# Four layers of linear attention and MLP on one Trainium2 core: the order of VectorE's first instructions, and three more row tiles turned by DMA

## The chip, the core and the metric

The kernel runs on one core of a Trainium2 chip. The core has TensorE (matrix products, into PSUM), VectorE, ScalarE and GpSimd (elementwise work), and SyncE, whose queue issues all DMAs of this kernel. The metric is the device time of one execution in microseconds (us). Every time in this text is in us unless another unit stands beside it.

## The reference

`x` is a bf16 array of 2048 rows by 576 columns. Two kinds of layer follow each other in the order A, B, A, B, each with a residual sum:

```python
def A(x, wqkv, wo):                      # 32 heads of 18 columns
    q, k, v = split(x @ wqkv)
    phi = lambda t: where(t > 0, t + 1, exp(t)) + 1e-6
    pq, pk = phi(q), phi(k)
    kv  = einsum("bhsd,bhse->bhde", pk, v)
    z   = einsum("bhsd->bhd", pk)
    num = einsum("bhqd,bhde->bhqe", pq, kv)
    den = einsum("bhqd,bhd->bhq", pq, z) + 1e-6
    return merge_heads(num / den) @ wo

def B(x, w1, b1, w2, b2):                # 576 -> 4608 -> 576
    y = layernorm(x)
    return gelu(y @ w1 + b1) @ w2 + b2

x = x + A(layernorm(x)); x = x + B(layernorm(x))
x = x + A(layernorm(x)); x = x + B(layernorm(x))
```

In the original, `A` gets `layernorm(x)`; B gets `layernorm(x)` too and applies a layernorm of its own to it, so B's rows are normalised twice. Both A layers use the same weights, and both B layers.

## The kernel before

The 2048 rows are 16 tiles of 128 rows. Layers are numbered from 1 in this text; in the code `li` counts from 0, so layer 1 is `li == 0`. Every product needs normalised rows with the model's columns on the partitions. That turned copy is `yT`, 128 partitions by 5 chunks by 2048 rows. A row tile becomes part of `yT` in three ways, named by `evac`: `"act"` (five TensorE transposes into PSUM, line 494, and a ScalarE copy, line 500, or for tiles 0 and 1 one copy each on ScalarE and VectorE, lines 497 and 498), `"xbar"` (one DMA transpose from SyncE's queue, line 483), and `"dma"` (VectorE's 32x32 transposes and a trip through DRAM, used for later layers).

`LNPipe` is a pipeline of normalisations. `feed` puts a tile in, and each `tick` takes every tile one stage on: stage 0 takes the statistics, on VectorE (two `bn_stats`, lines 391 and 392, an aggregate, line 398) or with `stats="act"` on ScalarE (a sum by Identity, line 371, a sum of squares by Square, line 381, and a small GpSimd step, line 384); stage 1 the inverse root, stage 2 the scale and shift, stage 3 the normalisation, stage 4 the turn. TensorE transposes are emitted by a tick with `transposes=1` only; a tick with `transposes=0` takes on everything else. `hold` is a number of ticks that a tile waits, and for tiles of a B layer `tp_at` is the number of the output tile (`state["wo"]`) ahead of which it isn't turned.

Layer 1 begins with a stretch written out by hand: the norms and keys of tiles 0 to 3 (`k_half(t, half)`: keys of one tile, half of the 576 columns; line 657), sums of rows times keys (`rows_by_keys`, line 699; its chunk 4 goes to a tile `k_tail` of its own), and the first two q products (`q_proj`, line 625: five matmuls for one group of heads and 512 rows). The products of q and k go through an exp on ScalarE (lines 544, 558, 559) and one or two VectorE instructions (546, 564, 566). TensorE's order is the order of emission (`pe_chain`). On the other engines the compiler's scheduler chooses, within data dependencies and manual edges. `in_order` lays such edges over VectorE's and ScalarE's first instructions by short names: `s2a`, `s2b`, `g2`, `u2` are the two statistics, the aggregate and the variance step of tile 2; `n2` its normalisation (line 440 for tiles 0 to 3, on VectorE; later tiles have it on GpSimd, line 436); `cd1` VectorE's copy of turned tile 1; `ma10` the VectorE step that finishes keys of tile 1, half 0; `e10` its exp and `ca1` ScalarE's copy.

Then a loop over tiles 4 to 15 repeats: keys of tile t, feed and tick (`pre_a1_layer0`, which also issues one piece of the weights for later, `late_pieces`), the row sums of tile t - 1, one q product, a tick without transposes. Tiles 0 to 7 (`XB = 8`) are turned by TensorE, tiles 8 to 15 by DMA. ScalarE takes the statistics of tiles 9, 12 and 15. The turn DMAs of layer 1 and all loads of weights are `chained`: SyncE issues them in order of emission.

The output stage of layer 1 is a loop over 16 output tiles: `wo_stage(t)` multiplies (ten matmuls, line 968, into one of two PSUM bank pairs), `residual` adds the input rows on VectorE (line 609) and stores the sum to DRAM from SyncE's queue (line 616). The first four sums are fed to the pipeline as layer 2's rows of block 0 (kind "B", normalised on GpSimd, line 457, into one of three ring buffers). They are turned by TensorE after output tiles 6, 10, 11 and 14. From output tile 12 on, each step issues one of the last three pieces of `w2` (`last_pieces`, 864 KB each). Layer 2's MLP begins with block 0, all of whose four row tiles its first product needs (line 1082).

Of the kernel before, what the change touches and what calls it, by code (L numbers as in the profile page):

```python
# [15 lines left out]
P = 128  # L16
NT = S // P
KD = 5
DPAD = KD * P
# [8 lines left out]
TPC = CB // P  # L28
# [8 lines left out]
def build(tc, A_x, A_wqkv, A_wo, B_w1, B_b1, B_w2, B_b2, out, dbg=None, n_layers=4):  # L37
    nc = tc.nc
    dbg = dbg or {}
    with ExitStack() as ctx:  # L40
# [90 lines left out]
        yT = const.tile([P, KD, S], BF16, name="yT")  # L131
# [3 lines left out]
        y_ring = [const.tile([P, DPAD], BF16, name=f"y_ring{i}") for i in range(NY)]  # L135
        key_eps = const.tile([P, 8], F32, name="key_eps")
        AHEAD = 4
        XB = 8
        turned = const.tile([P, D // 32, TPC, 32], BF16, name="turned")
        x_d = dpool.tile([NT, P, D], F32, name="x_d")  # L140
        yrow_d = dpool.tile([NCB, 4, TPC, 32, D], BF16, name="yrow_d")
# [197 lines left out]
        class LNPipe:  # L339
# [11 lines left out]
            def tick(self, transposes=1):  # L351
                land()
                for it in list(self.items):
                    st = it["stage"]
                    if st == 4 and it["evac"] not in ("dma", "xbar"):
                        if transposes == 0 or state["wo"] < it["tp_at"]:
                            continue
                        transposes -= 1
# [3 lines left out]
                    if st == -1:  # L362
                        xn = row_tile("xl")
                        load = nc.sync.dma_start(out=xn[:], in_=x_d[it["load"]])
                        if it["after"] is not None:
                            tc.add_manual_dep(load.ins, it["after"], NOSYNC, reason="loads give way")
                        it["xt"] = xn
                    elif st == 0 and it["stats"] == "act":
                        mv = it["mv"] = work.tile([P, 2], F32, name="ln_mv", bufs=6)
                        it["dump"] = blk.tile([P, D], BF16, name="ln_dump", tag="blk")  # L370
                        one = nc.scalar.activation(out=it["dump"][:], in_=it["xt"][:, 0:D], func=ACT.Identity,
                                                   scale=-1.0 / D, accum_out=mv[:, 0:1])
                        if it["after"] == "rden":
                            tc.add_manual_dep(one.ins, act_last["copy"], NOSYNC, reason="scalings first")
                        it["stage"] = 0.5
                        if it["kind"] == "B":
                            continue
                    if it["stage"] == 0.5:
                        u = it["u"] = work.tile([P, 1], F32, name="ln_u", bufs=4)
# [94 lines left out]
                    elif st == 4:  # L474
                        t = it["t"]
                        first_layer = it["kind"] == "A" and it["evac"] in ("act", "xbar")
                        y = it["xt"] if first_layer else it["y"]
                        if it["evac"] == "dma":
                            turn_rows(y, t, it["kind"])
                            self.items.remove(it)  # L480
                            continue
                        if it["evac"] == "xbar":
                            chained(nc.sync.dma_start_transpose(out=yT[:, :, t * P:(t + 1) * P], in_=y[:, 0:DPAD]))
                            self.items.remove(it)
                            continue
                        tp = ps_h.tile([P, 512], F32, name="tp", tag="h")
                        tp = tp[:, 0:DPAD // 2].bitcast(BF16).rearrange("p (k n) -> p k n", k=KD)
                        first = first_layer and t < 2
                        tp2 = tp
                        if first:  # L490
                            tp2 = ps_h.tile([P, 512], F32, name="tp2", tag="h")
                            tp2 = tp2[:, 0:DPAD // 2].bitcast(BF16).rearrange("p (k n) -> p k n", k=KD)
                        for k in range(KD):
                            pe(nc.tensor.transpose(out=(tp if k < 3 else tp2)[:, k, :], in_=y[:, k * P:(k + 1) * P],
                                                   identity=ident[:]))
                        if first:
                            named(f"ca{t}", nc.scalar.copy(out=yT[:, 0:3, t * P:(t + 1) * P], in_=tp[:, 0:3, :]))  # L497
                            named(f"cd{t}", nc.vector.tensor_copy(out=yT[:, 3:KD, t * P:(t + 1) * P], in_=tp2[:, 3:KD, :]))
                        elif it["evac"] == "act":
                            turned_tile = nc.scalar.copy(out=yT[:, :, t * P:(t + 1) * P], in_=tp)  # L500
                            act_last["turned"] = turned_tile.ins.name
                            if first_layer and t < 5:
                                named(f"ca{t}", turned_tile)
                            elif act_last["exp"] is not None:
                                tc.add_manual_dep(turned_tile.ins, act_last["exp"], NOSYNC, reason="keys go on first")
                        else:
                            nc.vector.tensor_copy(out=yT[:, :, t * P:(t + 1) * P], in_=tp)
                        self.items.remove(it)
                        continue
# [6 lines left out]
        lnp = LNPipe()  # L516
# [102 lines left out]
        def layer_A(li, next_kind, pre_a1=None):  # L619
# [237 lines left out]
            if li == 0:  # L857
# [5 lines left out]
                def feed_and_tick(t, n):  # L863
                    feed0(t, after=dve_last["phi"] if t > 5 else None)
                    for _ in range(n):
                        lnp.tick()
# [13 lines left out]
                k_half(3, 1)  # L880
                k_half(3, 0)
                q_proj(*q_left.pop(0))
                phi = q_proj(*q_left.pop(0), defer=True)
                feed_and_tick(5, 1)
                feed_and_tick(6, 2)
                phi(after=first_ones["ca4"].ins.name)
                in_order("s0a s0b g0 s1a s1b n0 g1 cd0 n1 s2a s2b g2 cd1 s3a ma00 n2 s3b g3 u3 ma10 s4a "
                         "n3 ma11 ma20 s4b ma21 g4 u4 ma01 s5a s5b g5 u5 ma30 ma31")
                in_order("ln0 re0 ln1 re1 ca0 e00 ca1 ln2 re2 e01 e10 ca2 e11 e20 e21 ca3 e31 e30 ca4")
                rows_by_keys(3, 0, (0, 1, 2, 3), done=False)  # L890
                for t in range(4):
                    rows_by_keys(t, 0, (4,))
                for t in range(4, NT):
                    keys(t)
                    pre_a1(t)
                    if t == 4:
                        lnp.tick()
                    masks(2)
                    if t > 4:
                        rows_by_keys(t - 1, 0)  # L900
                    q_proj(*q_left.pop(0), defer=True)(after=act_last["turned"])
                    lnp.tick(transposes=0)
                q_proj(*q_left.pop(0))
# [68 lines left out]
            def wo_stage(t):  # L972
                wo_products(t, range(wo_open[t][0] if t in wo_open else 0, G))
                wp = wo_open[t][1]
                xn = residual(li, t, wp[:, :, 0:HALF])
                if xn is not None and next_kind == "B" and t < TPC:
                    lnp.feed(xn, t, "B", "pool", "act", hold=(2, 5, 6, 8)[t] if li > 0 else (2, 8, 8, 10)[t], tp_at=6 + 2 * t if li > 0 else (6, 10, 11, 14)[t],
                             **(dict(after="sum") if t in (0, 3 if li > 0 else 2) else dict(stats="act", after="rden")))

            for t in range(AHEAD if li == 0 else AHEAD + 2):  # L980
# [14 lines left out]
            for t in range(NT):  # L995
# [17 lines left out]
                    quad_stage((t + 1) // 2, after=total)  # L1013
                if t == NT - 3:
                    warm_table(ACT.Gelu_apprx_tanh, act_last["copy"])
                if last_pieces and t >= NT - TPC:
                    last_pieces.pop(0)()
                state["wo"] = t
                lnp.tick()
                if t < 10:  # L1020
# [12 lines left out]
        class LayerB:  # L1033
# [70 lines left out]
            def run(self):  # L1104
# [7 lines left out]
                for c in range(NCB):  # L1112
# [2 lines left out]
                        tc.add_manual_dep(zero.ins, act_last["gelu"], NOSYNC, reason="not urgent")  # L1115
                    for g in range(self.done.get(c, 0), NGRP):
                        self.m1_group(c, g)
                        if g in (3, 5):
                            prefetch_xo(li, c * TPC + (g - 3) // 2, add_b2=True)
                        if g in (2, 3, 4, 5):  # L1120
                            feed_next(c, g - 2)
                        lnp.tick(transposes=0)
                        lnp.tick(transposes=0)
# [37 lines left out]

        def feed0(t, after=None):
            lnp.feed(x0_tiles.pop(t), t, "A", l0_norm_eng(t), "act" if t < XB else "xbar", after=after,
                     stats="act" if t >= XB and t % 3 == 0 else "dve")

        pe_chain.update(on=True, last=None)
        warm_pe(9)
# [7 lines left out]
        warm_pe(2)  # L1175

        def pre_a1_layer0(t):
            for ahead in (3, 4) if t == 4 else (4,):
                if t + ahead < NT:
                    feed0(t + ahead, after=dve_last["phi"])  # L1180
            lnp.tick()
            if late_pieces:
                late_pieces.pop(0)()
            if t == NT - 1:
                piece_b2_dma()
                while late_pieces:
                    late_pieces.pop(0)()
# [67 lines left out]
```

## Time and profile before

| what | value |
|---|---|
| median of 3 runs | 758.32 (758.32 to 758.42) |
| the profiled execution | 759.16 |
| its span, first to last instruction | 757.2 |
| granted TensorE clock, mean | 0.999 of full speed |
| TensorE busy | 750.6 (99% of the span) |
| VectorE, ScalarE, GpSimd busy | 261.3, 323.3, 114.9 |
| layer 1 up to its last q product, about | 0 to 60 |
| layer 1, sums and output stage | 60 to 100 |
| layer 2's first MLP product starts | 100.14 |

In rows of a timeline stand the start, the time from the first instruction's start to the last one's end, the engine, the line, the operation, what it writes and reads, its shape, and how many instructions are merged; in brackets the idle time of the engine before it and what ended that. Matmuls are pipelined, so what one costs TensorE is the distance from its start to the next start.

### The profile page before, as it was taken

The numbers are of one execution on the slowest core, as the hardware profiler recorded it, in microseconds if no ns is written. First come the engines' busy times: TensorE is split into PE (matmuls) and PEld (weight loads), VectorE is DVE, ScalarE is ACT, GpSimd is POOL, SyncE is SP. The second block draws the span as 40 slices with busy tenths as digits, with TensorE's granted clock in tenths as the row PEclk, the third lists the DMA queues.
The fourth block names the chain that finished last, engine by engine and source line by source line (L and its number), as shares of the span: only waits on it lengthen the run. The fifth ranks groups of instructions, "written<-read, shape, count | busy, mean of one in ns | idle before, by whom it ended". The sixth has DMA issues, their size and how long they took to land.

```text
span 757.2 us, 15677 instructions
## 1 busy us (share of the span) xinstructions
PE 750.6 (99%) x6555; PEld 484.7 (64%) x6555; DVE 261.3 (35%) x641; ACT 323.3 (43%) x722; POOL 114.9 (15%) x219
## 2 busy tenths in 40 slices
PE   8999999999999999999999999999999999999998
PEld 5677754774476457646777777457646754774476
DVE  7766824136034403401366567600230132000000
ACT  5767656105601640373057666660174036205600
POOL 4830313003010201200110004300020020001000
PEclk9999999999999999999999999999999999999999
DMA  8796692226313611411404147430240033011000
GB/s 241 172 246 159 200 350 65 71 65 182 82 40 94 166 51 48 121 54 32 127 24 118 32 137 256 173 83 16 87 106 17 16 126 83 9 32 56 1 9 24
DMA packets 83984, 75.20 MB, mean 99 GB/s; under 512 B 39882, under 2 KB 68554, under 8 KB 83914
## 3 DMA queue, kind: packets, MB, share of 16 engines
q1 hardware_dynamic: 83914, 74.21, 34.5%
q8 instruction: 51, 0.84, 0.5%
q14 instruction: 19, 0.16, 0.1%
HBM read 48.10 MB, written 24.77 MB: 96 GB/s over the span
## 4 chain that ended last, share of the span: by engine, by line
PE 95%; DMA 1%; ACT 1%; DVE 1%; POOL 1%; SPq 0%; issue 0%; POOLq 0%; DVEq 0%
PE m_ps L1144 36%; PE h_ps L1082 21%; PE hp_ps L1082 16%; PE q_ps L625 5%; PE k_ps L657 5%; PE k_ps L699 4%; PE wo_ps L968 3%; PE m_half L1144 1%; DMA xo<-x_d 1%; DMA x<-in_A_x_dram 1%; PE k_tail L699 0%; PE kv_ps L751 0%; ACT turned L846 0%; PE rden_ps L842 0%; PE den_ps L801 0%
## 5 line engine op out<-in xcount | busy, mean ns | idle before, releaser
L1144 PE MATMUL m_ps<-w_sb,hT 128*128 128x288 bf16 x2232 | 274.8, 286 | 0.0
L1144 PEld LDWEIGHTS <-hT 128*128 128x128 bf16 x2304 | 224.2, 98 | 60.4 <-issue 3.4
L1082 PEld LDWEIGHTS <-w_sb 64*128 64x128 bf16 x2304 | 124.5, 94 | 136.4 <-issue 1.9
L1082 PE MATMUL hp_ps<-yT,w_sb 64*128 64x512 bf16 x1152 | 178.0, 376 | 0.0
L1082 PE MATMUL h_ps<-yT,w_sb 64*128 64x512 bf16 x1152 | 148.0, 376 | 0.0
L1087 ACT COPY relay_sb<-relay_sb 128x1 f32<-128x1 f32 x144 | 28.5, 198 | 261.2 <-PE h_ps L1082 218.1
L1078 ACT ACTIVATE hT<-h_ps,b1T 128x512 bf16<-128x512 f32 x144 | 91.1, 683 | 43.8 <-PE h_ps L1082 43.8
L427 POOL TENSOR_TENSOR ln_rstd<-ln_u,neg_half 128x1 f32<-128x1 f32 x61 | 34.3, 563 | 412.3 <-DVE ln_u L409 209.4
L1078 ACT ACTIVATE hT<-hp_ps,b1T 128x512 bf16<-128x512 f32 x144 | 91.1, 692 | 0.0
L609 DVE TENSOR_TENSOR xbf<-m_ps,xo 128x576 bf16<-128x576 f32 x15 | 11.4, 757 | 212.9 <-PE m_ps L1144 212.9
L609 DVE TENSOR_TENSOR xo<-m_ps,xo 128x576 f32<-128x576 f32 x16 | 12.1, 757 | 168.2 <-PE m_ps L1144 168.2
L592 POOL TENSOR_TENSOR xo<-xo,b_bc 128x576 f32<-128x576 f32 x32 | 40.9, 1281 | 115.2 <-DMA xo<-x_d 85.3
L1082 PE MATMUL h_ps<-yT,w_tail 64*128 64x512 bf16 x144 | 54.1, 376 | 0.0
L1082 PE MATMUL hp_ps<-yT,w_tail 64*128 64x512 bf16 x144 | 54.1, 376 | 0.0
L625 PE MATMUL q_ps<-yT,wqkv_sb 128*126 128x512 bf16 (+1 forms) x200 | 49.4, 379 | 0.4 <-DVE pk L546 0.4
L657 PE MATMUL k_ps<-wqkv_sb,yT 128*128 128x288 bf16 x320 | 44.6, 286 | 0.3 <-DMA wqkv_sb<-in_A_wqkv_dram 0.2
L968 PE MATMUL wo_ps<-kvwo,pq 126*128 126x288 bf16 (+1 forms) x320 | 43.5, 286 | 0.6 <-DVE xo L609 0.4
L1082 PEld LDWEIGHTS <-w_tail 64*128 64x128 bf16 x288 | 27.1, 94 | 17.1
L657 PEld LDWEIGHTS <-yT 128*128 128x128 bf16 x320 | 31.0, 98 | 10.6 <-ACT yT L497 0.6
L968 PEld LDWEIGHTS <-pq 126*128 126x128 bf16 (+1 forms) x320 | 30.3, 97 | 9.6 <-issue 1.3
L558 ACT ACTIVATE phi_e<-q_ps 126x512 bf16<-126x512 f32 (+1 forms) x40 | 23.9, 596 | 23.6 <-PE q_ps L625 21.6
L625 PEld LDWEIGHTS <-wqkv_sb 128*126 128x126 bf16 (+1 forms) x200 | 25.7, 131 | 12.3 <-issue 1.0
(151 smaller groups left out, 562.5 us busy)
## 6 DMA issues: line engine op xcount, KB each, us to landing
xo<-x_d SPq DMA_DIRECT2D x48, 288.0 KB
x_d<-xo SPq DMA_DIRECT2D x32, 288.0 KB
xl<-x_d SPq DMA_DIRECT2D x24, 288.0 KB
y_d<-turned SPq DMA_DIRECT2D x40, 144.0 KB
w_sb<-in_B_w_dram SPq DMA_DIRECT2D x6, 864.0 KB
yT<-y_d SPq DMA_DIRECT2D x10, 512.0 KB
w_sb<-in_B_w_dram SPq DMA_DIRECT2D x9, 512.0 KB
x_d<-xn SPq DMA_DIRECT2D x16, 288.0 KB
```

Of the source, the lines that this page charges most:

```text
L427: nc.gpsimd.tensor_tensor(out=rstd[:], in0=it["u"][:], in1=neg_half[:], op=ALU.pow)
L558: exp = nc.scalar.activation(out=e_out, in_=ps_ap, func=ACT.Exp)
L592: nc.gpsimd.tensor_tensor(out=xo[:], in0=xo[:], in1=b2_bc[:], op=ALU.add)
L609: total = nc.vector.tensor_tensor(out=xn[:, cols].rearrange("p (h n) -> p h n", h=2), in0=halves, in1=xo[:, cols].rearrange("p (h n) -> p ...
L625: pe(nc.tensor.matmul(qp[0:GR[g], :], lhsT=wqkv_sb[:, k, GO[g]:GO[g] + GR[g]], rhs=yT[:, k, c * CA:(c + 1) * CA], start=(k == 0), stop=(k ...
L657: pe(nc.tensor.matmul(kp[:, 0:HALF], lhsT=yT[:, k, t * P:(t + 1) * P], rhs=wqkv_sb[:, k, D + half * HALF: D + (half + 1) * HALF], start=(k ...
L699: pe(nc.tensor.matmul(dst, lhsT=lhsT, rhs=pk, start=(t == 0), stop=(t == NT - 1)))
L968: pe(nc.tensor.matmul(wp[:, half, 0:HALF], lhsT=pq[(g, c)][0:GR[g], j * P:(j + 1) * P], rhs=kvwo[g][0:GR[g], half * HALF:(half + 1) * HALF ...
L1078: act_last["gelu"] = nc.scalar.activation(out=to, in_=ps, func=ACT.Gelu_apprx_tanh, bias=b1T[:, f:f + 1], scale=1.0).ins.name
L1082: mm = pe(nc.tensor.matmul(dst[n], lhsT=wt, rhs=mv, start=(seen[n] == 0), stop=(seen[n] == 8)))
L1087: relay = nc.scalar.copy(out=relay_sb[:, 1:2], in_=relay_sb[:, 0:1])
L1144: pe(nc.tensor.matmul(acc[half][:, 0:cols.stop - cols.start], lhsT=hT[f][:, j * P:(j + 1) * P], rhs=w2_sb[:, f, cols], start=(f == 0), sto ...
```

## The change

- `XB` goes from 8 to 7: tile 7 is turned by DMA. Its statistics move to ScalarE, and the rule `t % 3 == 1` in place of `t % 3 == 0` gives ScalarE the tiles 7, 10 and 13 instead of 9, 12 and 15.
- Tile 7 is fed ahead of the loop, with a tick without transposes, and without the edge that put its statistics behind VectorE's last key step. Tile 8 alone is fed at t = 4.
- The feeds and ticks of tiles 5 and 6 come ahead of the second q product instead of behind it, so tile 4 is turned between the first and the second.
- VectorE's order by hand is another one: among others `ma00` and `n2` go ahead of `s3a`, `ma01` moves up behind `ma10`, and the statistics of tiles 4 and 5 move down.
- The four `k_tail` products of tiles 0 to 3 come behind the keys of tile 4 instead of ahead of them.
- In layer 1's output stage, the rows of tiles 0 and 1 for layer 2's block 0 are turned by DMA (not `chained`) instead of TensorE, not ahead of output tiles 6 and 10. Tile 1's two statistics steps on ScalarE are emitted in one tick.
- The three last pieces of `w2` are issued with the first three groups of layer 2's first products instead of with output tiles 12 to 14.

```diff
-        XB = 8
+        XB = 7
...
                     st = it["stage"]
+                    if st == 4 and it["kind"] == "B" and it["evac"] == "xbar" and state["wo"] < it["tp_at"]:
+                        continue
                     if st == 4 and it["evac"] not in ("dma", "xbar"):
...
                         it["stage"] = 0.5
-                        if it["kind"] == "B":
+                        if it["kind"] == "B" and it["evac"] != "xbar":
                             continue
...
+                        if it["evac"] == "xbar" and it["kind"] == "B":
+                            nc.sync.dma_start_transpose(out=yT[:, :, t * P:(t + 1) * P], in_=y[:, 0:DPAD])
+                            self.items.remove(it)
+                            continue
                         if it["evac"] == "xbar":
...
                 q_proj(*q_left.pop(0))
-                phi = q_proj(*q_left.pop(0), defer=True)
                 feed_and_tick(5, 1)
                 feed_and_tick(6, 2)
+                phi = q_proj(*q_left.pop(0), defer=True)
+                feed0(7)
+                lnp.tick(transposes=0)
                 phi(after=first_ones["ca4"].ins.name)
-                in_order("s0a s0b g0 s1a s1b n0 g1 cd0 n1 s2a s2b g2 cd1 s3a ma00 n2 s3b g3 u3 ma10 s4a "
-                         "n3 ma11 ma20 s4b ma21 g4 u4 ma01 s5a s5b g5 u5 ma30 ma31")
+                in_order("s0a s0b g0 s1a s1b n0 g1 cd0 n1 s2a s2b g2 cd1 ma00 n2 s3a s3b g3 u3 ma10 ma01 n3 ma11 ma20 "
+                         "s4a s4b g4 u4 ma21 ma31 s5a ma30 s5b g5 u5")
                 in_order("ln0 re0 ln1 re1 ca0 e00 ca1 ln2 re2 e01 e10 ca2 e11 e20 e21 ca3 e31 e30 ca4")
                 rows_by_keys(3, 0, (0, 1, 2, 3), done=False)
-                for t in range(4):
-                    rows_by_keys(t, 0, (4,))
                 for t in range(4, NT):
                     keys(t)
                     pre_a1(t)
                     if t == 4:
-                        lnp.tick()
+                        lnp.tick(transposes=0)
                     masks(2)
                     if t > 4:
                         rows_by_keys(t - 1, 0)
+                    else:
+                        for one in range(4):
+                            rows_by_keys(one, 0, (4,))
                     q_proj(*q_left.pop(0), defer=True)(after=act_last["turned"])
...
-                    lnp.feed(xn, t, "B", "pool", "act", hold=(2, 5, 6, 8)[t] if li > 0 else (2, 8, 8, 10)[t], tp_at=6 + 2 * t if li > 0 else (6, 10, 11, 14)[t],
+                    lnp.feed(xn, t, "B", "pool", "xbar" if li == 0 and t < 2 else "act", hold=(2, 5, 6, 8)[t] if li > 0 else (2, 8, 8, 10)[t], tp_at=6 + 2 * t if li > 0 else (6, 10, 11, 14)[t],
...
-                if last_pieces and t >= NT - TPC:
-                    last_pieces.pop(0)()
...
                         self.m1_group(c, g)
+                        if last_pieces:
+                            last_pieces.pop(0)()
...
-                     stats="act" if t >= XB and t % 3 == 0 else "dve")
+                     stats="act" if t >= XB and t % 3 == 1 else "dve")
...
-            for ahead in (3, 4) if t == 4 else (4,):
-                if t + ahead < NT:
-                    feed0(t + ahead, after=dve_last["phi"])
+            if t + 4 < NT:
+                feed0(t + 4, after=dve_last["phi"])
```

## The prediction

> **What bounds the kernel now.** I read the page's shares and chain first.
>
> ```profile
> PE 750.6 (99%) x6555; PEld 484.7 (64%) x6555; DVE 261.3 (35%) x641; ACT 323.3 (43%) x722; POOL 114.9 (15%) x219
> ...
> PE 95%; DMA 1%; ACT 1%; DVE 1%; POOL 1%; SPq 0%; issue 0%; POOLq 0%; DVEq 0%
> ```
>
> TensorE is busy 750.6 of 757.2 us and is 95% of the chain, at a granted clock of 0.999. So only two things can shorten the run: fewer TensorE instructions, or its 6.6 us of idle time. The view of TensorE's waits over the whole span names most of the second:
>
> ```profile
> PE warm_ps L221 <- DVE y_ring L216: 1.3, 1, 1.3
> PE tp L494 <- DVE x L440: 0.6, 1, 0.6
> PE q_ps L625 <- DVE pk L546: 0.4, 1, 0.4
> PE wo_ps L968 <- DVE xo L609: 0.4, 1, 0.4
> PE tp L494 <- ACT phi_a L559: 0.2, 1, 0.2
> PE k_ps L657 <- DMA wqkv_sb<-in_A_wqkv_dram: 0.2, 1, 0.2
> ```
>
> The second, third and fifth lie where the diff works. TensorE's timeline (start, duration, instructions, idle time before) places them:
>
> ```profile
> 9.61 0.45 PE L494 MATMUL tp<-ident,x 128*128 128x128 bf16 x5 [0.62 <-DVE x L440]
> ...
> 16.88 0.44 PE L494 MATMUL tp<-ident,x 128*128 128x128 bf16 x5
> 17.15 0.66 PE L699 MATMUL k_ps<-pk,x 128*128 128x289 bf16 x4
> 17.65 0.66 PE L699 MATMUL k_tail<-pk,x 128*65 128x289 bf16 x4
> 18.14 1.39 PE L657 MATMUL k_ps<-wqkv_sb,yT 128*128 128x288 bf16 x10
> 19.36 0.44 PE L494 MATMUL tp<-ident,x 128*128 128x128 bf16 x5
> 20.20 1.24 PE L625 MATMUL q_ps<-yT,wqkv_sb 128*126 128x512 bf16 x5 [0.39 <-DVE pk L546]
> ...
> 26.19 0.44 PE L494 MATMUL tp<-ident,x 128*128 128x128 bf16 x5 [0.22 <-ACT phi_a L559]
> 26.47 0.29 PE L699 MATMUL k_tail<-pk,x 128*65 128x289 bf16 x1
> ...
> 28.16 1.39 PE L657 MATMUL k_ps<-wqkv_sb,yT 128*128 128x288 bf16 x10
> ```
>
> Matmuls overlap, so cost is start to start: a tile's five transposes hold TensorE 26.47 - 26.19 = 0.28 us. They are tiles 2, 4, 5 and 7 here; the last row is tile 7's keys. From 26.5 to 60 us no wait is listed: from there TensorE alone sets the pace, so whatever is gained before 28.16 stays.
>
> **First tiles.** The norm n2 sits behind s3a, which waits for tile 3's load, and behind ma00. VectorE runs s3a at 8.39, ma00 at 8.77, n2 at 9.13. In the new order ma00 follows cd1 (start 7.46, 0.29 long; ma00's exp ended at 7.59) and n2 needs only the exp that ends at 8.39, so it starts about 8.45: 0.68 earlier. The matmuls before it were issued until 8.82, so the whole 0.62 goes. Then s3a, s3b, g3, u3 run at 8.8 to 10.05, tile 3's norm about 0.25 earlier than its 11.02, in time. What is late next is tile 4, whose turn now goes ahead of the second q product. Its u4 ends near 13.3 (13.74 before); from there 15.66 - 13.74 = 1.92 us pass to the end of its GpSimd norm, so 15.2, while TensorE gets there at 15.18. I charge 0.1.
>
> **The q product at 20.20.** Moving four k_tail matmuls behind keys(4) puts 0.49 us of work into this 0.39 wait, but takes the same cover from tile 4's eviction (17.35 to 18.04, keys at 18.14); the turn being a whole q product earlier (1.08 us) replaces it. Taken alone this gains 0.39. Against it stands a new load on ScalarE: tile 7's statistics move there from VectorE. Their price is a row of ScalarE's timeline, tile 9's:
>
> ```profile
> 22.73 0.69 ACT L371 ACTIVATE ln_dump<-x 128x576 bf16<-128x576 bf16 x1
> 23.31 0.21 ACT L371 ACTIVATION_READ_ACCUMULATOR ln_dump<-x 128x1 f32 x1
> ...
> 24.26 0.81 ACT L381 ACTIVATE ln_dump<-x,ln_mv 128x576 bf16<-128x576 bf16 x1
> 24.94 0.23 ACT L381 ACTIVATION_READ_ACCUMULATOR ln_dump<-x,ln_mv 128x1 f32 x1
> ```
>
> About 0.67 + 0.77 = 1.44 us. ScalarE idles 0.89 before 14.30 and 0.67 before 15.99, then runs solid to 20.5. In those two gaps the statistics cost nothing; wholly behind 16 us they delay the exps that release q's banks by up to 1.44. I take the gaps, as the emission (before the second q's exps, with tile 7's load landed at 13.18 in the landing records) lies nearest to them.
>
> **Tile 7.** Its five transposes go, 0.28, and their wait, 0.22; ScalarE loses a 0.69 copy, and tile 9's statistics, which caused that wait, go to VectorE. In place comes one DMA turn on SyncE's queue, behind the first w1 piece and ahead of the second. Its cover: keys(7) comes at 28.16 less the 1.4 gained by then, 26.75. Tile 8's turn is the nearest row: issue 25.94, landed 28.68, 2.74 us; the worst is tile 11's, behind the wo weights: 34.67 to 39.73, 5.06 us, only 0.24 before keys(11) at 39.97. From the square's end through GpSimd (u, pow, nmr, norm: 26.73 to 28.85 for tile 9) take 2.2 us. So the square must end by 26.75 - 2.74 - 2.2 = 21.8, or 19.5 with the worst row; I expect 16 to 18. Cost nothing, at worst as in the slower rival below. The w1 pieces behind it are not read before 100 us.
>
> The Trainium skill (DMA: Bandwidth & Descriptors, "Latency and other measured facts") gives DMA transposes 261 GB/s with a non-contiguous middle dimension; by it the 160 KB turn would take an estimated 0.63 us, the limit would be 23.9, and the slower rival less likely. No row here shows 0.63 from issue to landing: the issue alone takes 1.21, and the trace decides.
>
> **Output stage.** Ten transposes go: 2 x 0.28 = 0.56. Two ScalarE copies go (0.69 each), off the path. Not all of 0.56 is kept. Product 7, at 87.39 behind the first turn, needs the bank pair of sum 5, whose row on VectorE is 86.38 + 0.75 = 87.13; product 11, at 93.31, that of sum 9, 92.34 + 0.74 = 93.08. I charge 0.15, so 0.41. The first turn's y is ready at 84.39; the second's at 92.14, so with 2.74 to 5.06 us it lands at 94.9 to 97.2, and block 0 starts near 99.6. Tile 3 overwrites the first ring buffer at 96.04, long after the first turn. On SyncE each turn takes 1.2 us of issue ahead of row stores and residual loads; the latter (issued 90.98 and 94.31, landed 94.19 and 97.50, used from 96.26 and 98.89) have 1.4 to 2 us to spare. The three last w2 pieces move into the MLP's first three groups, some 4 us each; the first product by them comes after nine groups. Nothing.
>
> **Sum.** 0.62 - 0.10 + 0.39 + 0.28 + 0.22 + 0.41 = 1.82 us. The profiled execution was 759.16 (span 757.2 and 1.96 around it), which would become 757.3; it lies 0.84 over the median 758.32, and from that I get 756.5. A difference of 0.2%, 1.5 us, is about what a measurement of this kernel can tell from none: 756.8. The most the start-to-start gaps allow (0.79, 0.56, 0.11 and 0.38 us, plus 0.28 and 0.56) is 2.7 us: 755.6.
>
> **Rivals.**
> - *ScalarE is late instead.* The statistics fall wholly or half between tile 4's copy and the second q's exps. For it: ScalarE is solid from 15.99 to 20.5, and tile 9's statistics did just that to an eviction at 25.5. Against: the gaps before 16. It costs 0.7 to 1.44 us, gain 0.4 to 1.1: 757.2 to 757.9.
> - *The turn of tile 11 is the new wait.* Its slack is 0.24 while TensorE comes 1.4 earlier; if the queue (DMA share 1.09 from 30 to 40 us) doesn't move along, TensorE loses up to 1.2 of the gain there: 757.7. Against: its issue followed its norm within 0.03 us, and that moves with TensorE.
> - *Slower: tile 7's DMA turn is late.* One wait before keys(7), and every later turn behind it. It decides when the square ends after 21.8; the run is slower by over 1.5 when keys(7) starts after 28.16 + 1.5 + 0.41 = 30.1, so with a square ending after 25.1, or after 22.8 with the 5.06 row: 760 to 761. For it: tile 9's square, with the same kind of emission, ended at 25.17. Against: tile 7 is emitted before the loop, an iteration and a half ahead of it.
> - *The order does nothing* (the schedule puts n2 where it was): only the 15 transposes and the 0.22 remain, 0.91: 757.4.
>
> **Chances.** The forecast 0.50 (its own range 755.6 to 756.8); ScalarE 0.20, tile 11 and the idle order 0.15 together, all within 0.2%; slower 0.15. Leaving out the slower rival and little else, the range is 755.5 to 758.9, its upper end being no gain and a turn late by about 0.5.
>
> **What would show it.** Right: no wait before tile 2's turn, which starts near 9.0; no tile 7 among the L494 rows, 45 of them up to 110 us instead of 60; keys(7) near 26.75; block 0 near 98.3, against 100.14; both statistics rows of tile 7 on ScalarE before 16. Wrong: a wait of TensorE for the DMA yT<-x or yT<-y_ring, for phi_a at the third q product, or for the sums at products 7 and 11 of over 0.2.

## The result: slower, and the profile after

The changed kernel takes 763.01 us (median of 7 runs, 760.64 to 765.16), the kernel before 758.42 beside it (7 runs, 758.32 to 758.99). The ratio is 1.0056, with an interval of 1.0038 to 1.0075. The forecast was 756.5 and a range up to 758.9, so the sign was wrong. The profiled execution took 763.62, its span is 761.7, and the mean granted clock 0.998.

Two pages of the profile answer to the first lines shown of before, shares and chain. TensorE's busy time didn't fall, although 15 transposes are gone, and its share of the chain did:

```profile
PE 751.8 (99%) x6540; PEld 484.1 (64%) x6540; DVE 261.8 (34%) x641; ACT 321.9 (42%) x719; POOL 115.4 (15%) x219
...
PE 93%; DVE 2%; DMA 2%; ACT 1%; issue 1%; POOL 1%; SPq 0%; DVEq 0%; POOLq 0%; ACTq 0%
```

TensorE's waits over the whole span of the changed kernel (total, times, longest), where two new lines stand on top:

```profile
PE wo_ps L977 <- DVE xn L615: 2.5, 1, 2.5
PE k_ps L663 <- DMA yT<-x: 2.1, 2, 1.9
PE warm_ps L221 <- DVE y_ring L216: 1.3, 1, 1.3
PE q_ps L631 <- DVE pk L552: 0.3, 1, 0.3
```

TensorE's timeline of the changed kernel (the lines have moved: keys are L663, the products of the output stage L977, layer 2's first product L1089):

```profile
8.90 0.45 PE L500 MATMUL tp<-ident,x 128*128 128x128 bf16 x5
...
19.45 1.24 PE L631 MATMUL q_ps<-yT,wqkv_sb 128*126 128x512 bf16 x5 [0.26 <-DVE pk L552]
...
26.76 1.39 PE L663 MATMUL k_ps<-wqkv_sb,yT 128*128 128x288 bf16 x10
...
30.14 1.40 PE L663 MATMUL k_ps<-wqkv_sb,yT 128*128 128x288 bf16 x10 [0.18 <-DMA yT<-x]
...
40.99 1.40 PE L663 MATMUL k_ps<-wqkv_sb,yT 128*128 128x288 bf16 x10 [1.91 <-DMA yT<-x]
...
94.05 5.52 PE L977 MATMUL wo_ps<-kvwo,pq 126*128 126x288 bf16 x30 [2.52 <-DVE xn L615]
...
105.00 1.04 PE L1089 MATMUL h_ps<-yT,w_sb 64*128 64x512 bf16 x8
```

Read as a ledger of starts, before to after: keys(7) 28.16 to 26.76, a gain of 1.40. Keys(11) 39.97 to 40.99, a loss of 1.02: so 2.42 us went between the two tiles, 1.91 of it in one wait for tile 11's turn and most of the rest ahead of keys(8), at 30.14. The row of 26 matmuls early in the output stage 77.22 to 78.25, still 1.03 late. Block 0 100.14 to 105.00, 4.86 late: another 3.83 went in the output stage. After it, nothing more is lost (span 4.5 longer).

**The output stage.** VectorE's row of the sum that TensorE waits for names its releaser, the landing of a store:

```profile
93.24 0.76 DVE L615 TENSOR_TENSOR xn<-wo_ps,xo_pair 128x576 f32<-128x576 f32 x1 [2.69 <-DMA x_d<-xn]
```

SyncE's timeline of the changed kernel shows why that store is late (L622 stores a sum's rows, L585 loads residual rows, L485 is the first turn for layer 2):

```profile
81.47 1.72 SPq L622 DMA_DIRECT2D x_d<-xn  x2
85.45 1.24 SPq L485 DMA_TRANSPOSE yT<-y_ring  x1
87.20 0.40 SPq L585 DMA_DIRECT2D xo_pair<-in_A_x_dram  x1
87.72 0.87 SPq L622 DMA_DIRECT2D x_d<-xn  x2
```

From 83.2 to 85.45 SyncE stands still: the turn is next in its queue, and GpSimd's last copy into `y_ring` ends at 85.42. The view of SyncE's waits has it as a line:

```profile
SPq L485 <- POOL y_ring L469: 2.2, 1, 2.2
```

Behind it stand a load of residual rows and the stores of sums 3 and 4 (counted from 0), which VectorE has done at 84.71 and 86.42. Before, these two were issued at 83.70 and 85.41; now at 87.72 and 88.21. By the landing records (the times at which a DMA's data is marked as arrived, sixteen marks for each DMA) the store of sum 4 landed at 88.04 before and at 93.15 now, and sum 7, which needs the row buffer that it frees, starts at 93.24; product 9, which needs the banks of sum 7, follows at 94.05.

The landing is 5.11 us later, and the queue's order is only a part of that: 1.03 is the lateness from layer 1, 1.77 the later place in the queue, and 2.31 a longer way from issue to landing, 4.93 in place of 2.62. Of that way the sixteen marks tell the end: fifteen are in by 91.73, the last comes 1.42 later. A 16 KB packet on a queue that fetches instructions ran through the DMA engines from 90.62 to 91.57. That it held up one engine's part of the store fits, as in the trace of before, where the packet came at 87.53 and the store of sum 5, issued at 87.15, has its last mark 1.21 late; but the records don't name the engine. The 30 matmuls behind the wait then take 5.52 us where a row of 30 took 3.92 earlier in this stage (at 85.68), and the windows by one microsecond say why: the third number from the end, ahead of the DMA's share and GB/s, is the granted clock.

```profile
94.00:95.00 1.00, 0.95 (x8) 0.70 (x8) 0.91 (x3) 0.99 (x3) 0.55 (x1) 0.91 0.18 71
95.00:96.00 1.00, 1.00 (x6) 0.63 (x5) 1.00 (x4) 0.47 (x2) 0.86 (x2) 0.50 0.36 21
96.00:97.00 1.00, 1.00 (x6) 0.63 (x5) 1.00 (x3) 0.00 (x0) 0.94 (x2) 0.50 0.82 217
```

The clock records hold 0.50 from 94.83 for 3.41 us, in which 1.7 us of work is lost. The stage's loss: 2.52 of waiting and 1.6 of half clock, less about 0.4 that the ten transposes give back, is 3.7 of the 3.83. This is the ledger of the profiled execution. By the mean clocks, half-clock stretches of this length (they leave 1 - 0.5 x 3.41 / 760 = 0.998) are in three of the seven runs, 762.1 to 764.2; the runs at 763.01 and 765.16 have 1.000 and 0.999 and must have lost their time otherwise.

**Tile 7's statistics** on ScalarE, from its timeline, are behind the second q's exps, not in the gaps before 16:

```profile
17.80 0.72 ACT L373 ACTIVATE ln_dump<-x 128x576 bf16<-128x576 bf16 x1
...
18.47 0.44 ACT L550 ACTIVATE phi_e<-k_ps 128x288 bf16<-128x288 f32 x1
18.76 0.81 ACT L383 ACTIVATE ln_dump<-x,ln_mv 128x576 bf16<-128x576 bf16 x1
```

### The profile page after: what moved, and what is told of

Its sections match the earlier page's. It is cut to its first block, busy times and chain, and to the rows that moved or that the text cites. A ratio compares the mean times of both kernels' runs of the same rounds, so it can differ in the third digit from the quotient of the medians.

```text
span 761.7 us, 15657 instructions
## 1 busy us (share of the span) xinstructions
PE 751.8 (99%) x6540; PEld 484.1 (64%) x6540; DVE 261.8 (34%) x641; ACT 321.9 (42%) x719; POOL 115.4 (15%) x219
## 4 chain that ended last, share of the span: by engine, by line
PE 93%; DVE 2%; DMA 2%; ACT 1%; issue 1%; POOL 1%; SPq 0%; DVEq 0%; POOLq 0%; ACTq 0%
PE m_ps L1153 36%; PE h_ps L1089 20%; PE hp_ps L1089 16%; PE q_ps L631 5%; PE k_ps L663 4%; PE k_ps L705 4%; PE wo_ps L977 3%; PE m_half L1153 1%; DMA yT<-x 1%; DMA x_d<-xn 1%; PE warm_ps L221 1%; PE kv_ps L757 0%; PE tp L500 0%; PE k_tail L705 0%; DVE xo L615 0%
## 5 line engine op out<-in xcount | busy, mean ns | idle before, releaser
L1089 PEld LDWEIGHTS <-w_sb 64*128 64x128 bf16 x2304 | 124.4, 94 | 136.7 <-issue 1.9
L1089 PE MATMUL hp_ps<-yT,w_sb 64*128 64x512 bf16 x1152 | 178.0, 376 | 0.0
L1089 PE MATMUL h_ps<-yT,w_sb 64*128 64x512 bf16 x1152 | 147.9, 376 | 0.0
L1089 PE MATMUL h_ps<-yT,w_tail 64*128 64x512 bf16 x144 | 54.1, 376 | 0.0
L1089 PE MATMUL hp_ps<-yT,w_tail 64*128 64x512 bf16 x144 | 54.1, 376 | 0.0
L977 PE MATMUL wo_ps<-kvwo,pq 126*128 126x288 bf16 (+1 forms) x320 | 44.7, 292 | 2.8 <-DVE xn L615 2.5
L663 PE MATMUL k_ps<-wqkv_sb,yT 128*128 128x288 bf16 x320 | 44.8, 286 | 2.1 <-DMA yT<-x 2.1
L977 PEld LDWEIGHTS <-pq 126*128 126x128 bf16 (+1 forms) x320 | 31.1, 99 | 12.9 <-issue 3.6
L663 PEld LDWEIGHTS <-yT 128*128 128x128 bf16 x320 | 30.6, 98 | 13.2 <-DMA yT<-x 3.0
L1089 PEld LDWEIGHTS <-w_tail 64*128 64x128 bf16 x288 | 27.1, 94 | 17.1
```

Source lines behind the costliest of these rows:

```text
L663: pe(nc.tensor.matmul(kp[:, 0:HALF], lhsT=yT[:, k, t * P:(t + 1) * P], rhs=wqkv_sb[:, k, D + half * HALF: D + (half + 1) * HALF], start=(k ...
L977: pe(nc.tensor.matmul(wp[:, half, 0:HALF], lhsT=pq[(g, c)][0:GR[g], j * P:(j + 1) * P], rhs=kvwo[g][0:GR[g], half * HALF:(half + 1) * HALF ...
L1089: mm = pe(nc.tensor.matmul(dst[n], lhsT=wt, rhs=mv, start=(seen[n] == 0), stop=(seen[n] == 8)))
```

## Experiments

Theories after the result: (1) in layer 1 the turns land late because they stand in a full DMA queue behind weight pieces, and TensorE, now earlier, reaches them first; (2) in the output stage the first turn's place in SyncE's queue delays stores and so row buffers; the rival to (2) is that the backlog of layer 1 alone makes it. Each kernel was timed beside the kernel before, whose medians were 758.55 (first four kernels), 758.82 (next four) and 758.37 (last four), with single runs from 757.9 to 760.8 and one of 763.2 in the first.

**Each part alone.** `l1_only` is the changed kernel with the output stage of before; `out_only` the reverse, layer 1 of before.

```diff
# l1_only, against the changed kernel
-    lnp.feed(xn, t, "B", "pool", "xbar" if li == 0 and t < 2 else "act", ...
+    lnp.feed(xn, t, "B", "pool", "act", ...
+                if last_pieces and t >= NT - TPC:
+                    last_pieces.pop(0)()
...
-                        if last_pieces:
-                            last_pieces.pop(0)()
```

> Layer 1's part of the change alone; the output stage and the w2 pieces as before. Theory (two losses that have nothing to do with each other; in layer 1 the turn of tile 11 lands late and takes back what the first tiles won): keys(7) start at 26.8, TensorE waits about 2 us for the DMA yT<-x before keys(11), no wait for xn in the output stage, the granted clock stays 1.00; layer 2's first product comes about 1.0 us later than before's 100.14, and the time is 759.4 (758.4 to 760.5). Rival (the output stage's wait follows from the backlog of layer 1's DMAs): the wait of 2.5 us for xn is here too, and the time is about 762.5.

Measured 758.33 (757.91 to 762.17, 12 runs), ratio 1.0005 (0.9988 to 1.0021); profiled 758.17. TensorE has no wait for a sum. Eight runs lie at 757.9 to 758.6, one at 759.5, and three at 761.9 to 762.2 with a mean clock of 0.997 to 0.998 where the others have 0.999 to 1.000. The profiled run is a near one, with little backlog of its own, so it doesn't decide on the rival to (2); its wait for tile 11's turn is 0.55:

```profile
39.30 1.40 PE L663 MATMUL k_ps<-wqkv_sb,yT 128*128 128x288 bf16 x10 [0.55 <-DMA yT<-x]
```

Keys(7) start at 26.70, 1.46 early; keys(11) only 0.67 early; block 0 at 99.59, 0.55 early.

> The output stage's part alone (tiles 0 and 1 turned by DMA, w2 pieces later); layer 1 as before. Theory (the first turn stands in SyncE's queue ahead of the stores of sums 3 and 4, waits there for its norm, and the late stores hold row buffers that sum 7 needs): a wait of 2 to 3 us for xn near 90 us, a stretch of half clock behind it, first product of layer 2 at 103 to 104, time 761 to 762.5. Rival (backlog of layer 1 is needed for it): no such wait, time 757.9, as the prediction's 0.41 us.

Measured 760.14 (759.52 to 760.82, 12 runs), ratio 1.0012 (1.0001 to 1.0023) against a spread of before that reaches 763.2; the medians differ by 1.59. Profiled 760.19. SyncE's, VectorE's and TensorE's timelines:

```profile
83.87 1.24 SPq L485 DMA_TRANSPOSE yT<-y_ring  x1
...
86.27 1.71 SPq L622 DMA_DIRECT2D x_d<-xn  x2
```

```profile
90.70 0.76 DVE L615 TENSOR_TENSOR xn<-wo_ps,xo_pair 128x576 f32<-128x576 f32 x1 [1.73 <-DMA x_d<-xn]
```

```profile
91.52 2.62 PE L974 MATMUL wo_ps<-kvwo,pq 126*128 126x288 bf16 x20 [1.56 <-DVE xn L615]
```

The same chain, turn, stores, sum, product, without any backlog from layer 1: the rival to (2) is refuted. Block 0 starts at 101.66, 1.52 late. The chain is shorter than expected, and behind 1.56 us of idleness the clock stays at 1.00. The landing records show what is missing: here the store of sum 4 takes 3.00 us, and its sixteen marks are all in by 90.61, 0.26 behind the fifteenth; the 16 KB packet had passed at 85.95, ahead of that store's issue at 87.61.

**The turn's place alone.** `turns_behind_stores` is the whole change; edges set each of the two turns, and the `w2` pieces, behind the latest store in SyncE's queue.

```diff
-    nc.sync.dma_start_transpose(out=yT[:, :, t * P:(t + 1) * P], in_=y[:, 0:DPAD])
+    turn = nc.sync.dma_start_transpose(out=yT[:, :, t * P:(t + 1) * P], in_=y[:, 0:DPAD])
+    tc.add_manual_dep(turn.ins, sp_last["store"], NOSYNC, reason="stores first")
...
     last_pieces.pop(0)()
+    tc.add_manual_dep(piece_of["w2"], sp_last["store"], NOSYNC, reason="stores first")
```

> The whole change, but in the output stage each of the two turns is ordered on SyncE behind the latest store (of sum 6 and of sum 10), and the w2 pieces behind the last store. Theory (the place in SyncE's queue is the cause): no wait for xn, clock 1.00, layer 1's loss of about 1 us stays, the transposes' 0.4 is won: 759.0 (758.2 to 760.0). Rival (a turn in the DMA queues slows the stores beside it, wherever it stands): a wait of over 1 us for xn stays, time 761 or more.

Measured 758.43 (757.65 to 761.95, 12 runs), ratio 1.0005 (0.9989 to 1.0021), where the changed kernel has 1.0056. Its median is that of before, but its runs lie far apart, and three of them, 761.5 to 762.0, have a mean clock of 0.998. In the profiled one (760.67) no wait for a sum is left, but one for a turn in layer 1, this time tile 10's:

```profile
38.91 1.40 PE L666 MATMUL k_ps<-wqkv_sb,yT 128*128 128x288 bf16 x10 [2.64 <-DMA yT<-x]
```

From the first output product to block 0 it takes 23.47 us (78.24 to 101.71), before 23.78 (76.36 to 100.14): without the delayed stores the ten transposes are worth 0.31.

**Layer 1: tile 7, the wo loads, the queue.** `t7_on_pe` is `l1_only` with tile 7 turned by TensorE after all (`t <= XB` in place of `t < XB` in `feed0`).

> As l1_only, but tile 7 is turned by TensorE; its statistics stay on ScalarE and the order of the first tiles stays the new one. Theory (the seventh tile's turn and the w1 piece that it holds back fill the DMA queue ahead of the wo weights and tile 11's turn): keys(11) wait under 0.9 us, so the time is 757.2 to 758.0, faster than l1_only by 1.5 or more. Rival (tile 11's turn is bound by the wo load alone, and TensorE merely arrives earlier at the same landing): the landing of tile 11's turn stays near 40 to 41 us, keys(11) start where they do in l1_only, time 758.5 to 759.5.

Measured 758.38 (757.69 to 759.68, 12 runs), ratio 0.9995 (0.9983 to 1.0006). The median is that of `l1_only`, not 1.5 better: what is not gained at tile 7 (keys at 27.11, 0.41 later) is mostly not lost by tile 11 either. A wait of 0.45 for tile 10's turn stands in place of the 0.55, keys(11) start at 39.42, 0.12 later than there, and block 0 at 99.59 as there. Only the far runs are gone, and three of twelve against none can be chance.

`l1_wo_last` is `l1_only`, `before_wo_last` the kernel before, `after_wo_last` the changed kernel, and `all_mended` is `turns_behind_stores`, each with the same edit, which puts the two `wo` loads behind all pieces of `w1` and so behind the last turn:

```diff
-        late_pieces = [(lambda i=i: piece_w1(i)) for i in range(4)] + [piece_wo] + \
-                      [(lambda i=i: piece_w1(i)) for i in range(4, 9)] + \
+        late_pieces = [(lambda i=i: piece_w1(i)) for i in range(9)] + [piece_wo] + \
```

> Layer 1's part alone, with the two loads of the wo weights moved on SyncE behind the last turn and the ninth w1 piece. Theory (the wo load, ahead of tile 11's turn, is what makes that turn and the next ones late, by an amount that differs from run to run): tile 11's turn lands within 3.5 us of its issue, no wait for yT<-x over 0.3 us, keys(11) start near 38.5, the runs lie within 0.6 us of each other, and the median is 757.0 (756.6 to 757.4). Rival (the queue is simply too full with one more turn and one more w1 piece): a wait of 0.5 us or more stays at one of keys(8) to keys(12), median 758 or more.

Measured 758.24 (757.58 to 760.57, 11 runs), ratio 0.9993 (0.9983 to 1.0002). The profiled run (758.79) still waits 1.27 us for tile 11's turn, issued 33.50 and landed 40.03, behind a `w1` piece that took from 31.73 to 39.26. No `wo` load was ahead of it: as the only cause these loads fall.

> The kernel before, with only the two wo loads moved behind the last turn. Theory: before has its spread of 758 to 760.5 on this chip from the same late turn, so the runs above 759 are gone and the median is 758.1 to 758.3; the first tiles' waits stay. Rival (the spread comes from elsewhere, such as the output stage): runs above 759 stay as frequent as in before.

Measured 758.50 (758.21 to 759.73, 11 runs), ratio 0.9998 (0.9989 to 1.0007): the edit by itself is worth nothing. Three of 11 runs lie above 759, of the kernel before 12 of 27: too few to say whether it narrows the spread.

> The whole change as it is, with the wo loads moved behind the last turn; the turns of the output stage stay ahead of the stores. Theory (two independent losses): layer 1's waits are gone, the wait for xn of 1.5 to 2.7 us stays, 758.5 to 760.5. Rival (the output stage's wait follows from the backlog that the wo load leaves): 756.6 as all_mended.

Measured 761.56 (759.80 to 762.60, 5 runs), ratio 1.0034 (1.0021 to 1.0046). Only 0.2 us of waiting for a turn is left, keys(11) start at 39.09, and yet the same 2.5 us for a sum and 3.41 us of half clock (from 92.8) follow. So the output stage's loss needs no loss ahead of it. The store of sum 4 again takes 4.93 us, its last mark 1.37 behind the fifteenth, with a 16 KB packet from 88.66 to 89.61.

> turns_behind_stores with the wo loads moved behind the last turn: the whole change without both losses. Theory: the prediction's sum of 1.82 us holds, 756.6 (756.2 to 757.0), runs within 0.6 us. Rival (a third loss is hidden behind these two): 757.5 or more.

Measured 757.39 (757.26 to 759.10, 11 runs), ratio 0.9988 (0.9979 to 0.9997): the best of all, and the only one whose interval lies below 1. It misses its expected 756.2 to 757.0 all the same, and its runs spread over 1.8 us. Waits and TensorE's rows in its profile (757.33):

```profile
PE warm_ps L221 <- DVE y_ring L216: 1.3, 1, 1.3
PE q_ps L633 <- DVE pk L554: 0.3, 1, 0.3
PE k_ps L665 <- DMA wqkv_sb<-in_A_wqkv_dram: 0.2, 1, 0.2
```

```profile
26.74 1.39 PE L665 MATMUL k_ps<-wqkv_sb,yT 128*128 128x288 bf16 x10
...
38.72 1.39 PE L665 MATMUL k_ps<-wqkv_sb,yT 128*128 128x288 bf16 x10
...
98.67 1.04 PE L1091 MATMUL h_ps<-yT,w_sb 64*128 64x512 bf16 x8
```

Neither new wait is there, block 0 is 1.47 early, and SyncE's order is now stores, then turn:

```profile
85.92 1.99 SPq L624 DMA_DIRECT2D x_d<-xn  x2
88.01 2.21 SPq L486 DMA_TRANSPOSE yT<-y_ring  x1
```

It has no room: tile 11's turn lands at 38.61 and is read at 38.72, the second turn of the output stage lands at 98.54 and is read from 98.67.

**What in the queue makes a turn late.** `l1_p1_early` is `l1_only` with two weight pieces at t = 4 in place of one, so that the `wo` loads come one tile earlier (the expectation below has them in their old place, which this edit doesn't do); `mended_p1_early` is the same in `all_mended`.

```diff
-            if late_pieces:
-                late_pieces.pop(0)()
+            for _ in range(2 if t == 4 else 1):
+                if late_pieces:
+                    late_pieces.pop(0)()
```

> Layer 1's part alone, with the first two w1 pieces issued ahead of tile 7's turn (as in before, where the second went out at 17.03 into a queue that then had nothing to do) and the wo loads in their old place. Theory (one w1 piece and one turn more in the crowded stretch of the DMA queue make the turns late): tile 8's turn lands near 28 instead of 29.2, tile 11's about 1.5 us earlier than in l1_only (near 37.8), the waits for yT<-x are under 0.3 us, median 757.3 (756.9 to 757.8). Rival (the lateness is a stall of the turn itself between 35 and 39 us, and the queue ahead of it doesn't matter): tile 11's turn still lands at 39 or later, median 758.2 or more.

Measured 761.57 (761.30 to 762.06, 5 runs), ratio 1.0041 (1.0027 to 1.0054). The `wo` loads are issued at 28.78 and 29.45, right behind tile 9's turn (27.53), and it is tile 9's that is late now, landed 35.00; tile 11's lands at 37.94. In every run the mean clock is 0.997 or 0.998. TensorE's row and two windows:

```profile
35.04 1.51 PE L663 MATMUL k_ps<-wqkv_sb,yT 128*128 128x288 bf16 x10 [2.06 <-DMA yT<-x]
```

```profile
36.00:37.00 1.00, 1.00 (x7) 0.69 (x6) 0.46 (x1) 1.00 (x4) 0.73 (x4) 0.59 1.15 319
37.00:38.00 1.00, 1.00 (x6) 0.62 (x4) 0.46 (x1) 0.99 (x3) 0.00 (x0) 0.50 1.16 340
```

> all_mended with the first two w1 pieces ahead of tile 7's turn. Theory: no wait for yT<-x in any run, so the runs above 758 of all_mended are gone: median 757.1 (756.6 to 757.4), all runs within 0.5 us. Rival (stall): as all_mended, 757.4 with runs up to 759.

Measured 758.44 (757.24 to 761.22, 11 runs), ratio 1.0001 (0.9992 to 1.0010). Here the `wo` loads come between the turns of tiles 14 and 15, and the turn that is most late is tile 14's: issued 41.81, landed 48.95, its keys behind a wait of 0.75. Twice, moving a load of weights moved the stall to another tile.

`mended_bare` is `all_mended` with no weights between the turns; all pieces come behind the last one (four at a time from t = 14 on, the `wo` loads first).

> all_mended, but no weights at all between the turns: all pieces go out behind the last turn, wo first. Theory of the crowded queue: every turn lands within 3.2 us of its issue, tile 11's near 36.7; no waits in layer 1 and no spread, median 757.0, unless the weights then come late for the wo products at 71 us or for layer 2 at 99 us. Rival (stall): the turn in flight between 34 and 37 us still takes over 4 us.

Measured 765.72 (764.50 to 766.15, 4 runs), ratio 1.0092 (1.0078 to 1.0106). In layer 1 it is the cleanest kernel of all: the turns of tiles 8 to 15 land 2.55 to 2.65 us after their issue, none is waited for, and keys come every 2.92 us from tile 9 on:

```profile
32.79 1.39 PE L665 MATMUL k_ps<-wqkv_sb,yT 128*128 128x288 bf16 x10
35.71 1.39 PE L665 MATMUL k_ps<-wqkv_sb,yT 128*128 128x288 bf16 x10
38.63 1.39 PE L665 MATMUL k_ps<-wqkv_sb,yT 128*128 128x288 bf16 x10
```

The weights then collide with the output stage. A load of residual rows is issued at 71.48 and lands at 82.29, VectorE and TensorE wait for it, and the clock is at half for 6.83 us from 81.3:

```profile
82.38 0.76 DVE L617 TENSOR_TENSOR xn<-wo_ps,xo_pair 128x576 f32<-128x576 f32 x1 [5.21 <-DMA xo_pair<-in_A_x_dram]
```

`l1_fetch_moved` tried a finer cause. In the landing records a 16 KB packet on a queue that fetches instructions passes through the DMA engines between 33 and 37 us. 36 warm-up matmuls of 128 columns in place of 9 of 512 put 27 matmuls and their weight loads ahead of it, to bring it earlier.

```diff
-        warm_pe(9)
+        warm_pe(36, cols=128)
```

> l1_only, with 36 warm-up matmuls of 128 columns in place of 9 of 512 at the very beginning: the same time on TensorE, but 54 more instructions. The idea: packets of a turn stall for 1.3 to 4.7 us between 35 and 39 us in each trace so far, and in each a 16 KB packet of the instruction queue (TensorE's next 256 instructions) lies 0 to 2.6 us ahead of that or in it. If the fetch is the cause, it moves some 4 us forward, to about 32 us, and the stalled packets of 256 bytes move with it to 32 to 35 us; tile 11's turn then lands earlier, and tile 9's or 10's later. If it isn't, the stalled packets stay at 35 to 38 us. The time says little: 757.5 to 759.

Measured 760.23 (758.73 to 760.77, 10 runs), ratio 1.0018 (1.0009 to 1.0027). The packet comes at 31.88 in place of 36.23, and the late turns are those of tiles 9 and 10 (27.51 to 34.19, 30.48 to 38.12) in place of 11. That the stall moved with the packet fits; but in `mended_bare` a packet at 33.20 delays nothing, and the two turns that moved above were late without one: tile 9's in `l1_p1_early` had landed (35.00) before the packet at 37.22, tile 14's in `mended_p1_early` was in flight from 41.81 to 48.95 with packets at 35.47 and 55.96. So a 16 KB packet isn't needed for a late turn. What each of packet, `wo` loads and `w1` pieces contributes in one execution stays open, as does why executions of one kernel differ.

## Why the prediction was wrong

**Right, by its own steps.** Tile 2's turn starts at 8.90 without a wait (near 9.0). Nine groups of transposes, 45, are left up to 110 us. Tile 7's turn, issued 22.99 and landed 26.39, costs nothing, and keys(7) start at 26.76 (26.75), so the sum 0.62 - 0.10 + 0.39 + 0.28 + 0.22 = 1.41 measured 1.40. That it fits to 0.01 is luck. Start to start, tile 2's turn gained 0.71 (9.61 to 8.90) in place of 0.52; from there to keys(5), 21.27 before and 20.60 now, nothing was gained in place of 0.39: 0.26 of that wait is still there, and the rest went in later starts; and from keys(5) to keys(7) 0.73 in place of 0.50. The slower rival on tile 7 didn't come. The 0.41 of the output stage showed as 0.31 in `turns_behind_stores`, where its stores weren't delayed, and as 0.24 in `all_mended`.

**Wrong with little effect.** Tile 7's statistics ran at 17.80 and 18.76, neither in the gaps before 16 nor between tile 4's copy and the second q's exps, where the ScalarE rival had them. The first ran ahead of the exp at 18.47, whose VectorE step ends at 19.40 and releases the q product at 19.45. So the statistics can have cost at most the 0.26 of that wait, not 0.7 to 1.44. From the square's end at 19.6 to the turn's issue at 22.99 it took 3.4 us in place of 2.2, and the turn landed 0.37 ahead of keys(7).

**The step that failed, worth 3.83 us in the profiled execution:** "On SyncE each turn takes 1.2 us of issue ahead of row stores and residual loads; the latter ... have 1.4 to 2 us to spare." The step costed the issue alone and checked the loads alone. The turn waits on SyncE for its data (2.2 us), two stores stand behind it, and a store's landing frees the row buffer of a later sum, for which TensorE then waits 2.52 us. "The first turn's y is ready at 84.39" was read as a time to land by, not as a time until which SyncE stands still. `out_only` shows it alone, with 1.56 us of waiting and 1.59 in the medians, and `turns_behind_stores` takes it away. Most of the rest of the 3.83 goes with the late last mark of one store, which `after_wo_last` has too and `out_only` hasn't, and with the half clock behind the longer wait; neither was on any list. (More row buffers, which would cut the chain at its other end, were not tried.)

**The step that was mis-sized, worth 2.42:** the rival "the turn of tile 11 is the new wait" was priced at up to 1.2, the gain that could be lost. Its argument against, that the issue moves with TensorE, is right (34.67 to 33.48) and doesn't help: the landing moved from 39.73 to 40.94, so 5.06 us of queue became 7.46. A turn in a full queue is not priced by its own row, and "whatever is gained before 28.16 stays" took the lack of a wait for room: tile 11's turn had 0.24. The Trainium skill's 261 GB/s (DMA: Bandwidth & Descriptors, "Latency and other measured facts"), by which the turn would take an estimated 0.63 us, is far from every row: 2.55 to 2.65 from issue to landing with the queue clear in `mended_bare`, 7.46 here.

With both steps mended the kernel is 1.43 us faster than before by the medians, by the interval 0.2 to 1.6, and so less than the 1.82 of the sum. `all_mended`'s block 0 is 1.47 early, by 0.35 less than summed: 0.18 of that is gone ahead of the output stage, whose first product starts at 75.13, 1.23 early in place of 1.41, and 0.17 in the stage. What took them isn't settled.

## What to carry to other kernels

A DMA that is moved to an in-order queue must be costed with the wait for its own data and with everything issued behind it, and stores count there, since their landing frees buffers. A gain ahead of a saturated queue is kept only if the landings behind it move too: compare the next landings with the new, earlier demand, not with the old one. Where a DMA replaces engine work, place it behind the work that others wait for.

## What the runs showed of the hardware

A short wait can cost more than itself, and where it falls decides. Behind idle times of 2.52 (the changed kernel) and 2.06 us (`l1_p1_early`) the granted clock fell to 0.50 for 3.41 us, worth 1.7 us more; behind 1.91 and 2.64 us (`turns_behind_stores`) it didn't, and behind 5.16 (`mended_bare`) it stayed there for 6.83, twice as long.

The clock records tell why a longer wait could be cheaper. The stretches between two changes of the clock are whole multiples of 3.413 us: until the fall 88.75 (26 of them) in the changed kernel, 30.72 (9) in `l1_p1_early`, 75.09 (22) in `mended_bare`. So from the first record on a trace can be cut into windows of that length. TensorE's idle time in the window ahead of the fall was 2.52, 2.06 and 3.26 us, and 1.90 in the next window of `mended_bare`, behind which the clock stayed low. A window's end split the 2.64 us into 0.95 and 1.68, and the 1.91 into 1.13 and 0.77. In the twelve traces that have clock records, every window with 1.90 us or more of idle time was followed by 0.50 and none with 1.73 or less; what lies between isn't shown.

The Trainium skill (TensorE: Matmul & The Clock Gate, Part 1) has the clock fall after at least one idle window of about 3.4 us, with a window that runs free. The length of 3.41 and the free run agree; the window didn't have to be idle as a whole here, so a wait below 3.4 us isn't safe.

In `l1_only` three of twelve runs (761.9 to 762.2) show the mean clock that such a half-clock stretch leaves, in `turns_behind_stores` three more, and one each of `mended_p1_early` (761.2) and of the kernel before (763.2); they weren't profiled, so its place in them is only argued.
